# Queries and keys of the later batches: float32 loads on the sync queue, a ScalarE cast and a transposing DMA in place of TensorE transposes

## The chip, the cores and the metric

One Trainium2 chip, one of its cores. The metric is the device time of one execution in microseconds (us). Before the change the median of four runs is 342.4 us (339.9 to 343.6). The profiled execution of the kernel before took 346 us and was slow (slow means here that a run is over 1.5% above the fastest of the same kernel). The stretches of it used below all ran at a granted TensorE clock of 1.00, so I compare periods there and not its total. (The granted clock is the share of full speed that the chip's throttle gave TensorE.)

## The reference

Block-sparse attention, then a gated feed-forward layer on its output (4 batches, 8 heads, 768 tokens, head size 64):

```python
scores = scale * np.matmul(q, k.transpose(0, 1, 3, 2))
mask = ...        # neighbours, first and last block, 3 sampled blocks per block of 32
attn = softmax(np.where(mask, scores, -1e9))
x = (attn @ v)    # heads side by side: [3072, 512]
return ((sigmoid(x @ w_gate) * (x @ w_val)) @ w_out)
```

Queries and keys are normal with a spread of 0.1, so every score is tiny and the softmax is almost flat. **The comparison with the reference hardly sees the keys and queries**.

## The kernel before

Tokens lie 8 to a partition (`(p j)`, 96 partitions). A turn brings one pair of heads to [128 = two heads x 64, tokens]: 16 TensorE transposes into PSUM, then copies that put the tokens back in order.

```python
def load_qk(b, p, nm):                       # POOL queue, casts to float16 on the way
    t = work.tile([96, 2, PJ, D], f16, tag=f"{nm}16", bufs=KQ[nm])
    nc.gpsimd.dma_start(t..., src[b, 2*p:2*p+2].rearrange("h (p j) d -> p h (j d)", j=PJ))

def turn(b, p, nm):
    pt = ps.tile([128, PJ, 96], f16, tag="st", bufs=2)         # PSUM, shared with the scores
    for j in range(PJ):
        for hd in range(2):
            nc.tensor.transpose(pt[hd*D:hd*D+D, j, :], src[:, hd, j, :], ident[0:96, 0:96])
    tok = pt.rearrange("p j (b a) -> p b a j", a=4)            # neighbours are 96 elements apart
    if nm == "k":
        nc.vector.tensor_copy(kT..., tok)
        nc.scalar.copy(kb..., kT...)  # twice
    else:
        nc.scalar.copy(z[0:D, :, 0], tok[0:D])
        nc.vector.tensor_copy(z[D:128, :, 1], tok[D:128])

def spread_v(b, hh):                         # a burst: 12 DMAs on the sync queue
    for a in range(4):
        for s in range(3):
            nc.sync.dma_start(v4b[hh][32*s:32*s+32, a:NB:4], va[b % 2][32*a:32*a+32, ...])

def ahead(w):         # what window w prepares: two windows a pair of heads, 8 windows a batch
    b, i = divmod(w, 2 * NP)
    ...               # turn of a key pair, of a query pair; at i == 4 and i == 6 a burst
    # [cut]
```

`load_batch(b)` issues all loads of a batch at once. The main loop runs the feed-forward layer of one half batch while it interleaves the attention of the next. In the traces below each engine and each queue is seen to take its instructions in program order (a transpose whose data was ready at 155.5 us is issued at 159.86 us, after the copies placed before it); this matters most below.

The softmax here doesn't subtract the row's maximum and nothing guards it: scores larger than these inputs give would overflow.

## Time and profile before

| | |
|---|---|
| time | 342.4 us |
| PE busy | 295.9 us of 344.2 |
| one batch in the steady part (sixth to twelfth write of an output tile) | 72.5 us |
| TensorE in that part | 70.6 us busy, at clock 1.00 |

In profiles PE is TensorE and PEld its weight loads, DVE is VectorE, ACT ScalarE, POOL GpSimd and SPq the sync queue. The page's first part gives the busy time of each engine, its share of the span and its instructions:

```profile
PE 295.9 (86%) x3584; PEld 188.6 (55%) x3584; DVE 197.9 (57%) x363; ACT 167.0 (49%) x275; POOL 130.4 (38%) x133
```

The table of stretches, for one steady batch period (columns: stretch, its length, then busy us and number of instructions of PE, PEld, DVE, ACT, POOL, then the granted clock, the DMA share and GB/s):

```profile
166.50:239.00 72.50, 70.59 (x898) 44.89 (x897) 45.24 (x79) 38.69 (x68) 30.60 (x30) 1.00 0.57 99
```

TensorE is the limit there: 97% of the period, while ACT is busy for 53% and DVE for 62%. The timeline of TensorE around one turn (start, duration, what):

```profile
134.50 0.33 PE L361 MATMUL st<-qz,kT 128*128 128x128 f16 x3
134.76 0.53 PE L280 MATMUL ptr<-ident,k 96*64 96x96 f16 x16
135.22 0.39 PE L496 MATMUL py<-wo,h 128*128 128x512 f16 x1
```

The turn holds TensorE from 134.76 to 135.22 us, so 0.46 us. The groups of instructions (busy us, mean ns of one, then idle time before them and what ended it) give the copies out of PSUM and the projections:

```profile
L471 PE MATMUL gv<-x,wg 128*128 128x384 f16 x384 | 80.3, 333 | 0.0
...
L302 DVE COPY qz<-ptr 64x768 f16<-64x768 f16 x16 | 15.4, 961 | 5.7 <-ACT qz L301 5.4
L286 DVE COPY kT<-ptr 128x768 f16<-128x768 f16 x16 | 15.2, 954 | 2.9 <-PE ptr L280 2.7
L301 ACT COPY qz<-ptr 64x768 f16<-64x768 f16 x16 | 12.7, 794 | 11.3 <-PE ptr L280 11.3
```

The timeline of the sync queue shows the two bursts of one batch's preparation:

```profile
130.47 8.47 SPq L148 DMA_DIRECT2D v<-va  x12
...
141.45 0.34 SPq L510 DMA_DIRECT2D out_dram<-y  x1
141.89 8.36 SPq L148 DMA_DIRECT2D v<-va  x12
```

For 20 us the queue is nearly always issuing. Before the change nothing urgent stands behind that.

### The profile page before, as it was taken

How to read it: one execution, taken by the hardware profiler on the slowest of the kernel's cores; microseconds unless marked ns; L12 is line 12 of the kernel's file. 1: busy time of each engine (PE TensorE's matmuls, PEld its weight loads, DVE VectorE, ACT ScalarE, POOL GpSimd, SP SyncE). 2: the span in 40 equal slices, each digit the busy share in tenths (PEclk: the TensorE clock that was granted, in tenths of full speed). 3: DMA queues.
4: the chain of work that ended last, by engine and by line, in shares of the span. 5: the costliest groups of instructions: out<-in, count | busy, mean ns of one | idle time of the engine just before them, and what ended most of it. 6: DMA issues, size and time to landing. Idle time of an engine off the chain costs nothing.

```text
span 344.2 us, 8514 instructions
## 1 busy us (share of the span) xinstructions
PE 295.9 (86%) x3584; PEld 188.6 (55%) x3584; DVE 197.9 (57%) x363; ACT 167.0 (49%) x275; POOL 130.4 (38%) x133
## 2 busy tenths in 40 slices
PE   2143479697899999999999999999999999999994
PEld 2132365465556666566556656665566566655541
DVE  5985543477476655865585646665766545543321
ACT  7935334455265636465455536553665364522210
POOL 8543669544442775323143944340332400000000
PEclk9999957899899999999999999999999999999999
DMA  9999989997202499740102997510120000001002
GB/s 123 164 187 209 161 124 158 203 222 161 51 2 64 55 184 197 173 96 32 30 3 64 156 225 167 132 56 5 30 64 32 0 33 32 33 9 54 30 32 92
DMA packets 61319, 33.10 MB, mean 96 GB/s; under 512 B 28128, under 2 KB 57696, under 8 KB 61280
## 3 DMA queue, kind: packets, MB, share of 16 engines
q0 software_dynamic: 36368, 14.16, 35.1%
q1 hardware_dynamic: 24912, 18.39, 21.6%
q8 instruction: 28, 0.46, 0.6%
q14 instruction: 11, 0.09, 0.1%
HBM read 28.57 MB, written 6.29 MB: 101 GB/s over the span
## 4 chain that ended last, share of the span: by engine, by line
PE 68%; DVE 15%; ACT 9%; issue 5%; DMA 1%; POOL 0%; DVEq 0%; ACTq 0%; POOLq 0%
PE gv L471 32%; PE py L496 16%; PE st L361 9%; ACT pt L386 7%; PE pv L414 6%; PE ptr L280 3%; DVE pt L396 3%; DVE qz L302 3%; PE ptx L459 2%; DVE kT L286 2%; DMA k<-in_k_dram 1%; DVE h L482 1%; DVE xs L449 1%; DVE v L146 1%; DVE y L505 1%
## 5 line engine op out<-in xcount | busy, mean ns | idle before, releaser
L386 ACT ACTIVATE pt<-st 128x1024 f16<-128x1024 f32 (+2 forms) x96 | 82.1, 863 | 61.8 <-PE st L361 60.1
L396 DVE TENSOR_TENSOR pt<-pt,mask 128x1024 f16<-128x1024 f16 x64 | 52.6, 822 | 59.3 <-ACT pt L386 58.9
L471 PE MATMUL gv<-x,wv 128*128 128x384 f16 x384 | 80.1, 332 | 2.6 <-DVE h L482 2.6
L482 DVE SCALAR_TENSOR_TENSOR h<-tg,gv 128x384 f16<-128x384 f32 x96 | 53.0, 552 | 50.9 <-PE gv L471 43.6
L480 ACT ACTIVATE tg<-gv 128x384 f32<-128x384 f32 x96 | 46.9, 489 | 69.9 <-PE gv L471 69.9
L471 PE MATMUL gv<-x,wg 128*128 128x384 f16 x384 | 80.3, 333 | 0.0
L496 PE MATMUL py<-wo,h 128*128 128x512 f16 x288 | 72.7, 380 | 0.0
L312 POOL INDIRECT_COPY kg<-kT,idx 128x608 uint32 (+1 forms) x32 | 36.1, 1130 | 96.4 <-DVE h L482 25.3
L326 POOL INDIRECT_COPY vg<-v,idx 128x768 uint32 (+1 forms) x32 | 45.4, 1419 | 45.3 <-issue 23.1
L471 PEld LDWEIGHTS <-wv 128*128 128x128 f16 x384 | 38.1, 99 | 30.7 <-issue 7.5
L361 PE MATMUL st<-qz,kT 128*128 128x128 f16 (+1 forms) x192 | 36.6, 255 | 14.4 <-DVE qz L302 14.4
L471 PEld LDWEIGHTS <-wg 128*128 128x128 f16 x384 | 34.9, 99 | 20.2 <-issue 2.1
L496 PEld LDWEIGHTS <-h 128*128 128x128 f16 x288 | 25.4, 98 | 22.5
L414 PEld LDWEIGHTS <-pt 96*32 96x32 f16 (+2 forms) x1280 | 30.9, 103 | 6.7 <-ACT pt L386 1.0
L361 PE MATMUL st<-qz,kg 128*128 128x64 f16 x352 | 22.1, 200 | 4.6 <-POOL kg L312 2.8
L361 PE MATMUL st<-qz,kb 128*128 128x256 f16 (+1 forms) x96 | 25.9, 285 | 0.0
L414 PE MATMUL pv<-va,pt 128*64 128x65 f16 (+1 forms) x384 | 24.3, 200 | 0.8 <-ACT pt L386 0.8
L361 PEld LDWEIGHTS <-kg 128*128 128x128 f16 x352 | 19.2, 103 | 9.8 <-POOL kg L312 3.0
L505 DVE TENSOR_SCALAR y<-py 128x512 f32<-128x512 f32 x24 | 16.5, 689 | 8.6 <-PE py L496 8.6
L130 POOL DMA_DIRECT2D va<-in_v_dram x24 | 21.2, 906 | 0.0
L361 PEld LDWEIGHTS <-kb 128*128 128x128 f16 x96 | 9.9, 103 | 18.6 <-issue 13.9
L361 PEld LDWEIGHTS <-kT 128*128 128x128 f16 x192 | 15.9, 102 | 7.6 <-DVE qz L302 1.7
(56 smaller groups left out, 246.9 us busy)
## 6 DMA issues: line engine op xcount, KB each, us to landing
v<-va SPq DMA_DIRECT2D x90, 99.0 KB, 2.7
out_dram<-y SPq DMA_DIRECT2D x20, 256.0 KB, 2.0
k<-in_k_dram POOLq DMA_DIRECT2D x16, 192.0 KB, 5.4
va<-in_v_dram POOLq DMA_DIRECT2D x24, 128.0 KB, 5.6
q<-in_q_dram POOLq DMA_DIRECT2D x16, 192.0 KB, 5.7
wg<-in_moe_w_gate_dram POOLq DMA_DIRECT2D x3, 512.0 KB, 5.6
wv<-in_moe_w_val_dram POOLq DMA_DIRECT2D x3, 512.0 KB, 7.4
wo<-in_moe_w_out_dram POOLq DMA_DIRECT2D x3, 512.0 KB, 10.2
```

Source lines behind the costliest of these rows:

```text
L130: nc.gpsimd.dma_start(va[b % 2][:, m, :, 0:D], v[b, :, m * 128 : m * 128 + 128].rearrange("h p d -> p h d"),)
L312: nc.gpsimd.indirect_copy(words(t, BLK // 2)[:, 0:n], words(kT[b, p], BLK // 2), idx[:, half, 0 : 3 - half], i_know_this_is_slow=True,)
L326: nc.gpsimd.indirect_copy(words(t, VE // 2)[:, 0 : 2 * n, 0 : D // 2], words(v4[p // 2][:, p % 2 * 2 * VE : p % 2 * 2 * VE + 6528], D // 2 ...
L361: nc.tensor.matmul(st[:, col : col + n], keys, qs, start=True, stop=True)
L386: nc.scalar.activation(pt[:, 0:n], st[:, 0:n], AF.Exp, scale=SCALE)
L396: nc.vector.tensor_tensor(pp, pp, mk.unsqueeze(2).to_broadcast([128, nt, 2, nq]), op=ALU.mult)
L414: nc.tensor.matmul(pvv[rows, t % 3, hd, :], probs[w, x][0:k, c : c + n], val[:, 0:65], start=first[0], stop=False, skip_group_check=True, ...
L471: nc.tensor.matmul(t, w[:, i, f * 128 : (f + 1) * 128], xT[g, i], start=(i == 0), stop=(i == NP - 1),)
L480: nc.scalar.activation(tg, pgs.pop((g, f)), AF.Tanh, scale=0.5)
L482: nc.vector.scalar_tensor_tensor(h_, tg, 1.0, pvv_.pop((g, f)), op0=ALU.add, op1=ALU.mult)
L496: nc.tensor.matmul(pys[g, tt], hts[g, f][:, tt * 128 : (tt + 1) * 128], wo[:, f], start=(f == 0), stop=(f == NF - 1),)
L505: nc.vector.tensor_scalar_mul(y, pys.pop((g, tt)), 0.5)
```

## The change

It means to free TensorE of 24 of its 32 turns. Batches 1 to 3 are loaded as float32 by the sync queue, cast by ScalarE into pair order, and transposed by a DMA from SBUF to SBUF; load, cast and turn are one window apart. The core of the diff:

```diff
+    def load_raw(b, p, nm):
+        t = work.tile([96, 2, PJ, D], f32, tag="raw", bufs=4, name="raw")
+        nc.sync.dma_start(..., src[b, 2*p:2*p+2].rearrange("h (p j) d -> p h (j d)", j=PJ))
+    def flip(b, p, nm):
+        c = work.tile([96, PJ, 2, D], f16, tag="cast", bufs=2, name="cast")
+        nc.scalar.copy(c, raw.pop((nm, b, p)).rearrange("p h j d -> p j h d"))
+        t = work.tile([128, PJ, 96], f16, tag="turned", bufs=2, name="turned")
+        nc.sync.dma_start_transpose(t, c.rearrange("p j h d -> p (j h d)"))
     def turn(b, p, nm):
+        if b:
+            pt = turned.pop((nm, b, p))       # the copies below now read SBUF
+        else:                                 # as before
-            [128, 1024 if x < 2 else 640], f16, tag=f"pt{x // 2}", bufs=5 - x // 2, name="pt"
+            [128, 1024 if x < 2 else 640], f16, tag=f"pt{x // 2}", bufs=5 - 2 * (x // 2), name="pt"
     def ahead(w):
+        if i == 2 and b + 1 < B:
+            r.append(lambda: load_v(b + 1))
+        later(5, "k", turn); later(4, "k", flip); later(3, "k", load_raw)
         if b + 1 < B:
             if i == 4:
                 r.append(lambda: (spread_v(b + 1, 0), second_v(b + 1, 0)))
             if i == 6:
                 r.append(lambda: spread_v(b + 1, 1))
         # [cut]
+        later(7, "q", turn); later(6, "q", flip); later(5, "q", load_raw)
     # [cut: load_batch goes; before the main loop come load_v(1) and two load_raw]
```

## The prediction

> **What bounds the kernel now.** TensorE. The page gives PE 295.9 us busy of 344.2 (86%); the chain of waits is 68% PE. From 100 to 280 us the table of stretches shows PE busy 19.1 to 20.0 us of every 20, DVE 11 to 14, ACT 10 to 11; PE's own waits in 100 to 300 us sum to about 5 us. A half batch (projections of one half beside attention of the next) takes 36.2 us there. Idle PE lies mostly before 60 us, where batch 0 is prepared; that part keeps its TensorE transposes.
>
> **Removed.** 24 of 32 turns (16 transposes each). By the timeline a turn occupies 0.46 us of PE from its first start to the next instruction's (134.76 to 135.22, 144.60 to 145.06) in the PE-bound stretch: 24 x 0.46 = 11 us, the whole possible gain (3.2%). Also 24 cast loads on the POOL queue (not critical), and the PSUM slot each turn held until DVE (0.96 us) or ACT and DVE (0.79 + 0.96) had copied it.
>
> **Added.**
> - ACT: 24 casts of 96x1024 from float32. The zero cast in the trace takes 0.86 ns per element, so about 1.06 us each, 25 us in all (estimate); not a bound, but a cast can delay a tanh or exp that PE needs within 1 to 2 us: 2 to 4 us of PE stalls.
> - SP queue: 24 loads (0.6 us each, as its other issues) and 24 transposes. No trace shows a transposing DMA. The Trainium skill ("DMA: Bandwidth & Descriptors", Latency and other measured facts) gives 261 GB/s as effective, so 192 KB moves in under 1 us beside the 2 to 3 us which the trace shows for any SP copy; estimate 3 to 5 us to landing, 1 to 2 us of issue.
> - DVE: the same copies, now from SBUF. The skill ("VectorE: DVE Perf Modes", What auto-detection actually checks) lets a single-source SBUF copy run at 2x; kT copies may fall from 0.96 to 0.5 us.
>
> **The critical point is the order on the SP queue.** Per batch it already issues two bursts of 12 value copies and 3 more (130.5 to 150.2 us). A turn follows its cast by 5 to 9 us, but the transpose of the second key pair queues behind the first burst, the first query pair's behind the second. I work out landings 0 to 4 us late in each place. DVE and ACT run in order, so a late turn holds h and tanh, and PE stops 1 to 2 us later. Six such places give back 0 to 15 us; middle, about 4.
>
> **Sum.** 343 - 11 + 3 (casts) + 4 (late turns) - 1 (DVE and PSUM relief) = 338 us. Range 327 (no stalls) to 354 (transposes of 6 us or more). Faster by over 2%: 0.40; within 2%: 0.34; slower by over 2%: 0.26.
>
> **What would show each step.** PE busy down some 15 us by the page's overlapping count, ptr matmuls 512 to 128; ACT busy up 25 us; transposes landing in 3 to 5 us; half-batch period 34.5 to 36 us. Stalls show as DVE kT or ACT and DVE qz copies waiting on the transposing DMA, and PE gv waiting on DVE h, at 75 to 90, 140 to 155 and 210 to 225 us.
>
> **What would make it wrong.** A transpose that costs much more on the SP queue or in the DMA engines (every turn late, y stores too: 360 us or more); a transpose under 2.5 us with a light burst (331); ACT waits for raw loads held behind the bursts.

## The result

| | before | the change |
|---|---|---|
| median of 4 runs | 342.35 us | 384.17 us |
| range | 339.9 to 343.6 | 383.3 to 386.3 |

The ratio is 1.124 (95% interval 1.116 to 1.132), so the change is 12% slower. Here and below a ratio is the mean time of one kernel's fast runs over that of the other's of the same rounds, so it is not quite the ratio of the medians quoted. The outputs are right.

The page's first part, and the groups that answer to those shown before, all of the change:

```profile
PE 299.4 (78%) x3200; PEld 186.6 (49%) x3200; DVE 192.9 (50%) x363; ACT 193.4 (51%) x299; POOL 118.9 (31%) x109
```

```profile
L496 PE MATMUL gv<-x,wg 128*128 128x384 f16 x384 | 85.8, 350 | 6.0 <-ACT tg L505 5.8
...
L145 ACT CAST cast<-raw 96x1024 f16<-96x1024 f32 x24 | 24.9, 1038 | 4.1 <-DMA raw<-in_q_dram 2.8 <-DMA raw<-in_k_dram 1.3
...
L326 ACT COPY qz<-turned 64x768 f16<-64x768 f16 x12 | 18.0, 1503 | 9.2 <-DMA turned<-cast 9.2
...
L327 DVE COPY qz<-turned 64x768 f16<-64x768 f16 x12 | 12.2, 1014 | 6.7 <-DMA turned<-cast 6.4
...
L311 DVE COPY kT<-turned 128x768 f16<-128x768 f16 x12 | 10.5, 871 | 15.0 <-DMA turned<-cast 15.0
```

Three things stand out. The 384 transposes (24 turns of 16) are gone from PE's count, and yet PE is busy 3.5 us longer: the same projection matmul takes 350 ns and not 333. ScalarE's query copy takes 1.50 us from SBUF against 0.79 us from PSUM. And the copies now wait for the transposing DMA. Its own cost is not to blame: it lands in a median of 3.1 us and holds the queue for 1.26 us, as predicted.

The sync queue of the change in the preparation of batch 2, by its timeline:

```profile
149.73 8.06 SPq L170 DMA_DIRECT2D v<-va  x12
...
159.15 0.60 SPq L180 DMA_DIRECT2D vb<-va  x1
159.86 1.75 SPq L147 DMA_TRANSPOSE turned<-cast  x1
161.71 0.53 SPq L535 DMA_DIRECT2D out_dram<-y  x1
162.29 0.41 SPq L137 DMA_DIRECT2D raw<-in_k_dram  x1
...
169.53 9.06 SPq L170 DMA_DIRECT2D v<-va  x12
178.70 1.30 SPq L147 DMA_TRANSPOSE turned<-cast  x1
180.04 0.58 SPq L137 DMA_DIRECT2D raw<-in_q_dram  x1
```

What the engines do meanwhile, from the timeline of all engines (in brackets: idle time before, and what ended it):

```profile
154.44 1.03 ACT L145 CAST cast<-raw 96x1024 f16<-96x1024 f32 x1
...
163.42 0.81 DVE L311 COPY kT<-turned 128x768 f16<-128x768 f16 x1 [3.35 <-DMA turned<-cast]
164.26 0.46 ACT L316 COPY kb<-kT 128x320 f16<-128x320 f16 x1 [4.98 <-DVE kT L311]
166.52 1.04 ACT L145 CAST cast<-raw 96x1024 f16<-96x1024 f32 x1 [0.52 <-DMA raw<-in_k_dram]
167.56 0.49 PE L484 MATMUL ptx<-ident,xs 128*128 128x128 f16 x3 [3.96 <-ACT cast L145]
...
181.56 1.49 ACT L326 COPY qz<-turned 64x768 f16<-64x768 f16 x1 [2.65 <-DMA turned<-cast]
184.07 1.04 ACT L145 CAST cast<-raw 96x1024 f16<-96x1024 f32 x1 [0.63 <-DMA raw<-in_q_dram]
185.02 0.69 ACT L411 ACTIVATE pt<-st 128x640 f16<-128x640 f32 x1
185.77 0.32 PE L439 MATMUL pv<-va,pt 128*64 128x65 f16 x3 [3.58 <-ACT pt L411]
```

Read it from the top. The cast is done at 155.5 us, but the queue is in its first burst and the three value copies behind it, so the transpose is issued at 159.86 and VectorE, which had come to the key copy, stands until 163.42. ScalarE stands behind VectorE for 4.98 us, and TensorE for 3.96 us. (The bracket names the cast, which ended last by the profile's count; the operand itself, `xs`, is VectorE's, written at 167.5 us behind that same key copy.) The second burst does it again, with one more link: the load issued at 180.04 holds a cast until 184.07, behind that cast stands an exp, and TensorE stands 3.58 us for the exp. Each such wait is short because the one before it has already eaten the time.

A stop costs TensorE more than its length. The table of stretches around the second stop, again of the change (the clock is the third number from the end):

```profile
180.00:185.00 5.00, 2.19 (x24) 1.35 (x21) 1.50 (x2) 2.81 (x3) 1.43 (x1) 0.97 0.94 208
185.00:190.00 5.00, 3.35 (x44) 2.27 (x45) 1.11 (x3) 0.93 (x3) 0.00 (x0) 0.50 0.56 121
190.00:195.00 5.00, 5.00 (x26) 2.50 (x25) 2.53 (x4) 0.85 (x3) 0.00 (x0) 0.85 0.15 38
```

The Trainium skill ("TensorE: Matmul & The Clock Gate", the part on the HAM clock gate) says that an idle window of about 3.4 us drops the array to half its clock until it has been busy for about as long. This trace agrees that a stop halves the clock, but not in both lengths: in the stop of 3.58 us the granted clock falls to 0.50 at 184.7 us, 2.5 us after the stop began, and stays there for 6.8 us, to 191.5 us; a stop of 3.08 us, from 267.77 us, does the same. Over the period 192.20 to 277.40 us, which holds the preparation of batch 3 with stops of 4.09 and 3.08 us in the same two places, the clock is 0.92, where before it is 1.00.

The period from the sixth to the twelfth output tile, read off VectorE's timeline, goes from 72.5 us (166.52 to 238.97) to 85.2 us (192.23 to 277.44), 12.8 us more. It holds the preparation of batch 3; the stops shown above, of batch 2, lie before it. Three batches are prepared this way, and 3 x 12.8 = 38 us is nearly the whole difference of 42 us. (The sixth tile, after two preparations, already comes 25.7 us later, twice 12.8; that figure leans on the slow profile of the kernel before.) After the last preparation nothing differs: from the twelfth to the eighteenth tile both take 69 us.

### The profile page after: what moved, and what is told of

Same layout as the page of the kernel before. It is cut to its first block, busy times and chain, and to the rows that moved or that the text cites. A ratio compares the mean times of both kernels' runs of the same rounds, so it can differ in the third digit from the quotient of the medians.

```text
span 382.6 us, 7839 instructions
## 1 busy us (share of the span) xinstructions
PE 299.4 (78%) x3200; PEld 186.6 (49%) x3200; DVE 192.9 (50%) x363; ACT 193.4 (51%) x299; POOL 118.9 (31%) x109
## 4 chain that ended last, share of the span: by engine, by line
PE 45%; DVE 15%; DMA 13%; ACT 12%; issue 8%; SPq 5%; POOL 0%; DVEq 0%; ACTq 0%; POOLq 0%
PE gv L496 21%; PE py L521 12%; ACT pt L411 7%; DMA turned<-cast 7%; PE st L386 5%; PE pv L439 4%; DMA raw<-in_q_dram 3%; DVE kT L311 3%; DVE qz L327 3%; SPq L170 2%; DVE pt L421 2%; PE ptx L484 2%; DVE xs L474 2%; SPq L147 1%; DMA pair<-in_k_dram 1%
## 5 line engine op out<-in xcount | busy, mean ns | idle before, releaser
L496 PE MATMUL gv<-x,wg 128*128 128x384 f16 x384 | 85.8, 350 | 6.0 <-ACT tg L505 5.8
L496 PE MATMUL gv<-x,wv 128*128 128x384 f16 x384 | 84.2, 345 | 4.0 <-DVE h L507 3.9
L421 DVE TENSOR_TENSOR pt<-pt,mask 128x1024 f16<-128x1024 f16 x64 | 47.2, 739 | 57.0 <-ACT pt L411 57.0
L521 PE MATMUL py<-wo,h 128*128 128x512 f16 x288 | 75.8, 392 | 0.0
L496 PEld LDWEIGHTS <-wg 128*128 128x128 f16 x384 | 37.5, 104 | 31.9 <-issue 13.9
L439 PE MATMUL pv<-va,pt 128*64 128x65 f16 (+1 forms) x384 | 25.2, 204 | 12.8 <-ACT pt L411 12.8
L484 PE MATMUL ptx<-ident,xs 128*128 128x128 f16 x96 | 12.5, 249 | 25.5 <-DVE xs L474 21.5
L145 ACT CAST cast<-raw 96x1024 f16<-96x1024 f32 x24 | 24.9, 1038 | 4.1 <-DMA raw<-in_q_dram 2.8
L316 ACT COPY kb<-kT 128x320 f16<-128x320 f16 x16 | 7.3, 457 | 31.0 <-DVE kT L311 31.0
L326 ACT COPY qz<-turned 64x768 f16<-64x768 f16 x12 | 18.0, 1503 | 9.2 <-DMA turned<-cast 9.2
L484 PEld LDWEIGHTS <-xs 128*128 128x128 f16 x96 | 6.9, 106 | 31.9 <-DVE xs L474 30.6
```

The costliest lines, as they stand in the source:

```text
L145: nc.scalar.copy(c, raw.pop((nm, b, p)).rearrange("p h j d -> p j h d"))
L421: nc.vector.tensor_tensor(pp, pp, mk.unsqueeze(2).to_broadcast([128, nt, 2, nq]), op=ALU.mult)
L439: nc.tensor.matmul(pvv[rows, t % 3, hd, :], probs[w, x][0:k, c : c + n], val[:, 0:65], start=first[0], stop=False, skip_group_check=True, ...
L484: nc.tensor.transpose(pt[:, t, :], x[:, t, :], ident)
L496: nc.tensor.matmul(t, w[:, i, f * 128 : (f + 1) * 128], xT[g, i], start=(i == 0), stop=(i == NP - 1),)
L521: nc.tensor.matmul(pys[g, tt], hts[g, f][:, tt * 128 : (tt + 1) * 128], wo[:, f], start=(f == 0), stop=(f == NF - 1),)
```

## The experiments

Theory A: the loads, casts and transposes are late, because loads and transposes stand behind the bursts on the sync queue. Theory B: the added work itself (25 us of casts, slower copies, DMA traffic) costs. All times are medians; the ratio is to the kernel before in the same rounds. "Period" is the sixth to twelfth output tile of the profiled run; in brackets where that run was slow.

| run | what | us | ratio | period |
|---|---|---|---|---|
| before | | 342.4 | | 72.5 |
| change | | 384.2 | 1.124 | 85.2 |
| e1 | turns wait for no transpose (wrong result) | 380.1 | 1.122 | 84.1 |
| e2 | no loads, casts, transposes (wrong result) | 340.3 | 0.998 | 71.7 |
| e3 | casts, but TensorE transposes | 354.5 | 1.043 | 74.6 |
| e4 | bursts in pieces | 350.2 | 1.031 | 72.8 |
| e5 | e2, copies in source order | 374.0 | 1.101 | 82.0 |
| e6 | e4 + e5's copies + later weight load | 384.4 | 1.129 | 86.0 |
| e7 | float32 loads on the POOL queue | 390.5 | 1.145 | 81.3 |
| e8 | e1 + e7 (wrong result) | 376.6 | 1.098 | (81.2) |
| e9 | e2, contiguous copies (wrong result) | 331.3 | 0.974 | 68.8 |
| e10 | e4 + later weight load | 346.6 | 1.014 | (73.1) |
| e11 | e10 + tokens loaded so that copies are contiguous | 346.1 | 1.017 | 71.3 |
| e12 | e11 with casting POOL loads | 341.6 | 1.001 | 69.4 |
| e13 | all work done, nothing waits for it (wrong result) | 342.6 | 1.005 | 72.5 |
| e14 | e12 for batches 2 and 3 only | 335.4 | 0.986 | 69.7 |
| e15 | before, with 8 wide TensorE transposes | 353.2 | 1.033 | 75.1 |

### First round: e1 to e4

e1 lets every later turn read one fixed tile; the transposes go into a tile nobody reads (here, in e8 and in e13 with one buffer in place of two). e2 has in addition a bare `return` in `load_raw` and `flip`, so loads, casts and transposes are gone.

```diff
-            pt = turned.pop((nm, b, p))
+            pt = fixed                        # filled once, from batch 0
```

> Wrong result on purpose: every later turn reads one fixed tile (real data of batch 0), while the loads, casts and transposing DMAs all still run, into a tile that nobody reads. Theory A (turns wait for transposes that land late behind the bursts on the SP queue): the waits on the transposing DMA go, so most of the loss goes: 335 to 350 us. Theory B (the added ScalarE work, 25 us of casts and 9 us of slower query copies, delays exp and tanh): nothing of that changes, so 370 us or more.

Measured 380.1 us. Read naively, theory A is dead. But the waits of e1 (us in all, times, longest) show that the time merely moved one link up:

```profile
ACT cast L146 <- DMA raw<-in_k_dram: 14.6, 4, 4.1
ACT cast L146 <- DMA raw<-in_q_dram: 12.7, 5, 4.3
```

In the change the casts waited 4.1 us in all for their loads; here it is 27 us. The loads stand behind the same bursts, and a cast that waits holds ScalarE just as well as a late turn. So e1 did not separate the theories.

> Wrong result on purpose: as e1, but no loads, casts or transposing DMAs of queries and keys after the first batch at all. What is left is TensorE without its 24 turns and the copies from SBUF. Theory A and B both expect the whole possible gain: about 331 us (343 less 11). If it stays above 350, something else in the change costs (the slower ScalarE copy from SBUF, the smaller buffer pool, the moved value loads).

Measured 340.3 us: no gain at all, although TensorE had 11 us less to do. Neither theory expected that; the text had named the slower copies as one candidate. e5 and e9 follow it up.

e3 keeps the loads and casts and transposes the cast tile with TensorE:

```diff
-        nc.sync.dma_start_transpose(t, c.rearrange("p j h d -> p (j h d)"))
+                    nc.tensor.transpose(pt[hd*D:hd*D+D, j, :], src[:, j, hd, :], ident[0:96, 0:96])
```

> The float32 loads and ScalarE casts stay, but TensorE transposes the cast tile as before, so no transposing DMA and copies from PSUM. Correct result. Theory A: near before plus a few us of casts, 343 to 352 us. Theory B: the casts alone cost most of it, 365 us or more.

Measured 354.5 us, a little over the range of A and far under B's. The period is 2.1 us longer than before; one wait of a cast for its load, 6.8 us, lies in the start.

e4 changes only what the sync queue issues when. Each burst becomes pieces, and the three extra value copies move to the last window of the batch:

```diff
-            if i == 4:
-                r.append(lambda: (spread_v(b + 1, 0), second_v(b + 1, 0)))
-            if i == 6:
-                r.append(lambda: spread_v(b + 1, 1))
+        if b + 1 < B and i >= 4:
+            hh, a0 = divmod(i - 4, 2)
+            pieces = [lambda a=a: spread_v(b + 1, hh, part=(a,)) for a in (2 * a0, 2 * a0 + 1)]
+        # at i = 4, 5 around the gathers; at i = 6, 7 after the query's flip and load
```

> The change with its value-copy bursts cut in pieces of 3 DMAs, spread over four windows and placed so that each transposing DMA finds at most two pieces ahead of it; everything else as in the change. Correct result. Theory A: the late turns of the second key pair and first query pair are no longer late, 350 to 365 us. Theory B: about 380 us.

Measured 350.2 us, 34 us won back by order alone, with every byte, cast and transpose still there. Its sync queue, for comparison with that of the change:

```profile
138.17 3.87 SPq L170 DMA_DIRECT2D v<-va  x6
142.86 1.24 SPq L147 DMA_TRANSPOSE turned<-cast  x1
144.15 0.58 SPq L137 DMA_DIRECT2D raw<-in_k_dram  x1
145.49 0.37 SPq L535 DMA_DIRECT2D out_dram<-y  x1
145.90 4.64 SPq L170 DMA_DIRECT2D v<-va  x6
```

The period is 72.8 us, 12.4 less than the change's. A 8.8 us stop of TensorE is left in the preparation of batch 1, where a transpose lands after 11.8 us beside the output-weight loads.

### Second round: e5 to e8

e5 (on top of e2) and e6 (on top of e4) walk the copies in the order of their source; e6 also issues the output-weight loads later, as e10 below:

```diff
-            nc.scalar.copy(z[0:D, :, 0], tok[0:D])
+            nc.scalar.copy(zj[0:D, 0], pj[0:D])     # reads neighbours, writes 8 elements apart
```

> e2 (wrong result on purpose: one fixed tile, no loads, casts or transposing DMAs) with the copies out of the turned tile walked in the order of their source, so that they read neighbouring elements. e2 came out at 340 us and not at 331; in the change the ScalarE query copy takes 1.50 us from SBUF against 0.79 us from PSUM. If that strided read from SBUF is what ate the floor's gain, the copy falls to about 0.85 us and the run to 330 to 336 us. If not, 339 to 341 us, and the loss sits elsewhere.

> e4 (split bursts, 350 us) with the copies of e5 and with the three output-weight loads moved from before the first group to the fifth to seventh window, because in e4 one transposing DMA took 11.8 us to land beside them and TensorE stood 8.8 us. Correct result. If order on the SP queue, that collision and the slow copy are the whole loss: 332 to 338 us. If the casts and the DMA traffic cost more than that: 341 us or more.

Both missed, in the wrong direction: 374.0 and 384.4 us. Neighbouring reads were bought with scattered writes, and those are far worse. The group of instructions in e5:

```profile
L327 ACT COPY qz<-fixed 64x768 f16<-64x768 f16 x12 | 41.8, 3483 | 0.0
L305 DVE COPY kT<-fixed 128x768 f16<-128x768 f16 x12 | 27.0, 2250 | 0.0
```

As a mend it failed, but it is a clean measurement of something else: 24 us more on ScalarE (12 x 1.97) and 27 us more on VectorE made e2 34 us longer, with TensorE's work unchanged. Both engines are only half busy; their time counts all the same, because what TensorE waits for stands behind it.

e7 moves the float32 loads to the POOL queue, e8 does e1 and e7 together:

```diff
-        nc.sync.dma_start(        # in load_raw
+        nc.gpsimd.dma_start(
```

> The change with only its float32 loads moved from the SP queue to the POOL queue; bursts as in the change. Correct result. Casts then no longer wait behind bursts, but the transposes still do. If the two ways of being late (cast waits for its load, turn waits for its transpose) cover for each other, this alone helps little, as e1 alone did: 368 to 382 us. If late loads were the one cause: about 345 us.

> e1 and e7 together (wrong result on purpose: turns read a fixed tile; float32 loads on the POOL queue). Neither casts nor turns can then wait behind a burst, with all work still done. If lateness behind the bursts is the cause: 340 to 352 us. If the added load on ScalarE and the DMA engines is: 370 us or more.

e7 was even slower than the change (390.5 us) and over its range; its steady period is 81.3 us, 4 less than the change's, but it loses more before that, up to the sixth tile. e8 came to 376.6 us, near what theory B expected (two of its four runs are slow; the fast ones took 371.3 and 376.1 us). But its waits, in a slow profile, again show casts held: 14.3 us for the transposing DMA, because a cast needs a buffer that a transpose still reads, and 13.0 us for loads that now stand on the POOL queue between its gathers (the copies that collect the sampled blocks). The two runs therefore settle nothing between A and B; they show how many ways the chain has to be late.

### Third round: e9 to e12

e9 is e2 with copies that read and write neighbours, and so leave the tokens in a wrong order:

```diff
-            nc.scalar.copy(z[0:D, :, 0], tok[0:D])
+                pj = pt.rearrange("p j n -> p (j n)").rearrange("p (b r) -> p b r", r=BLK)
+                nc.scalar.copy(zz[0:D, :, 0], pj[0:D])      # VectorE's two copies likewise
```

> e2 (wrong result on purpose, one fixed tile, nothing loaded or transposed) with copies that read and write neighbouring elements (tokens in a wrong order, also on purpose). e5 showed that walking the copies in source order makes their scattered writes far slower (3.48 us) and the run 34 us longer, so copies on ScalarE and VectorE do count. If the scattered 2-byte reads of the change (1.50 us) ate the gain in e2: copies near 0.86 us on ScalarE and 0.5 us on VectorE, and 328 to 335 us. If not: 338 to 341 us.

Measured 331.3 us, ratio 0.974: nearly the whole possible gain that the prediction had worked out (10 of 11 us by the medians; 3.7 of 3.7 us a period). Its copies, by group, with those of e2 after them:

```profile
L325 ACT COPY qz<-fixed 64x768 f16<-64x768 f16 x12 | 9.9, 824 | 0.0
...
L305 DVE COPY kT<-fixed 128x768 f16<-128x768 f16 x12 | 5.7, 477 | 0.0
```

```profile
L319 ACT COPY qz<-fixed 64x768 f16<-64x768 f16 x12 | 18.1, 1510 | 0.0
...
L304 DVE COPY kT<-fixed 128x768 f16<-128x768 f16 x12 | 13.0, 1087 | 0.0
```

So reading single float16 elements 192 bytes apart from SBUF ate the gain of the freed TensorE: 71.7 against 68.8 us a period. (Before the change ScalarE read at the same distance from PSUM in 0.79 us. e9's copies on VectorE are shorter than those before the change too, 0.48 against 0.95 us, so its gain is that of freed turns and short copies together.)

e10 moves only the output-weight loads of e4, out of the way of the first transposes (`if 5 <= w < 8: load_wo(w - 5)` in `ahead`); e11 loads tokens `(j p)`, so that the transposing DMA delivers them in order and, for keys, straight into their final tile; e12 has the POOL queue load and cast:

```diff
-            src[b, 2*p:2*p+2].rearrange("h (p j) d -> p h (j d)", j=PJ),
+            src[b, 2*p:2*p+2].rearrange("h (j p) d -> p (h j) d", j=PJ),     # e11: rows of 256 bytes
-        nc.scalar.copy(c, raw.pop((nm, b, p)).rearrange("p h j d -> p j h d"))
+            nc.gpsimd.dma_start(t[:, :, hd], src[b, 2*p+hd].rearrange("(j p) d -> p j d", j=PJ))  # e12
```

> e4 (split bursts, 350 us) with only the output-weight loads moved to the fifth to seventh window; copies as in the change. Correct result. e4 lost 8.8 us where a transposing DMA took 11.8 us beside those loads: 340 to 346 us if that collision is the cause, 349 to 352 us if the stall only moves.

> e10 with tokens loaded so that the transposing DMA gives them in order: loads of 256-byte rows, keys transposed straight into their final tile (no VectorE key copy), query copies of neighbouring elements. Casts stay on ScalarE. Correct result. Worked out per batch of 72.4 us before: less 3.7 for TensorE, plus about 2 for the casts, nothing for copies: 334 to 341 us; above 345 us if the loads of short rows come late.

> e11 without ScalarE casts: the POOL queue loads with a cast as before the change, two DMAs a tile, straight into pair order; the sync queue then only transposes. Correct result. If the casts and copies are all that is left of the loss: 330 to 337 us, better than before. If the POOL queue's extra issues delay its gathers: 340 us or more.

e10: 346.6 us, a little over its range; of the 8.8 us stop, 3.6 us were won in the median (6 us by the ratios, which leave out e10's slow run), and several stops of 2 to 3 us took its place. e11: 346.1 us, above its range, by the branch that the expectation named: its casts waited 15.5 us for the queries' short-row loads. e12, which also takes back the smaller probability pool, as e14 does: 341.6 us, equal to before. Its steady period is 69.4 us, 3 better than before, but it loses that in the preparation of batch 1, with stops of TensorE of 4.0 and 4.5 us.

### Fourth round: e13 to e15

By then the prediction was known to be wrong and no run had cleanly separated lateness from load. e13 does: everything is still loaded, cast and transposed, in the order of the change, and nothing waits for it.

```diff
-            pt = turned.pop((nm, b, p))
+            pt = fixed
-        nc.scalar.copy(c, raw.pop((nm, b, p)).rearrange("p h j d -> p j h d"))
+        nc.scalar.copy(c, some...)            # same shape, read from the weights as float32
-        nc.sync.dma_start_transpose(t, c.rearrange("p j h d -> p (j h d)"))
+        nc.sync.dma_start_transpose(t, still.rearrange("p j h d -> p (j h d)"))
```

> The change with all its added work done and nothing waiting for it (wrong result on purpose): turns read one fixed tile, casts read other data that is long there, the transposing DMAs read a fixed tile and write one that nobody reads, the float32 loads land in tiles that nobody reads; order on every queue as in the change. If lateness (casts and turns held behind the bursts) is the cause of what e4 won: e2's 340 us plus some 6 us for the casts, 343 to 351 us. If the added work itself (ScalarE, DMA traffic) is: 370 us or more.

Measured 342.6 us, even a little under the range. Its row for one period:

```profile
163.50:236.00 72.50, 66.46 (x770) 41.95 (x769) 43.24 (x78) 46.80 (x76) 25.55 (x22) 1.00 0.84 142
```

The row to hold beside it is that of the change:

```profile
192.20:277.40 85.20, 71.83 (x769) 44.10 (x768) 44.85 (x78) 47.44 (x76) 26.23 (x22) 0.92 0.69 121
```

Same matmuls, same ScalarE work, but 12.7 us between them, 13.4 us of idle TensorE (85.2 less 71.8) against 6.0, and clock 0.92 against 1.00. So lateness is the cause of the loss, as theory A has it. Of theory B's list, casts, loads and transposes together cost 0.8 us a period (72.5 against e2's 71.7); the slower copies, which e2 has too, cost the 2.9 us that e9 shows, and that is most of what the freed TensorE gains. e4, where every dependence is in place, has a period of 72.8 us: nearly all of the 12.7 us goes away by the order of the sync queue alone.

e14 keeps TensorE's transposes for batch 1 and does e12's for batches 2 and 3:

```diff
-                if 0 <= p < NP and 0 < b2 < B:
+                if 0 <= p < NP and 0 < b2 < B and (b2 > 1 or f is turn):
-        if b:
+        if b > 1:                             # in turn
+    load_qk(1, 0, "k"); load_qk(1, 0, "q"); load_v(1); ...      # batch 1 as before
```

> e12 for batches 2 and 3 only; batch 1 is loaded and transposed by TensorE as before. Correct result. In e12 the period from batch 1's to batch 2's first stored edge tile was 67.8 us against 72.4 us before, but batch 1, prepared beside the weight loads, stood still for some 15 us. If that is all: 341 less twice 4.6, 330 to 335 us, faster than before by 2 to 3%. If a transposing DMA is late in the other batches too: 338 us or more.

Measured 335.4 us, ratio 0.986 (0.983 to 0.989): the one right version that beats both kernels, by 1.4%, a little short of the range. The interval is clear of 1. The 67.8 us that the expectation quotes was read off the issue of stores, which the sync queue itself shifts; by the writes of output tiles e12's period is 69.4 us, so the gain to be had was 3 and not 4.6 us a batch.

e15 asks whether TensorE can be spared otherwise: the loads of the kernel before are written in pair order, so that 8 transposes of 128 columns do.

> The rival way to save TensorE time: before, with its cast loads written into pair order (two DMAs a tile on the POOL queue), so that a turn is 8 transposes of 128 columns instead of 16 of 64; no transposing DMA. Correct result. A turn should fall from 0.46 us to about 0.3 us of TensorE: 336 to 340 us; above 342 us if short-row writes make the loads late.

Measured 353.2 us, a miss. The loads now take two issues a tile on the POOL queue, which is in order too: it issues loads from 54.5 to 74.2 us, a gather stands behind them, and TensorE stands 14.3 us for that gather. What the wide transposes are worth was not separated from that.

## Why the prediction was wrong

**Right.** The place: "the transpose of the second key pair queues behind the first burst, the first query pair's behind the second", with VectorE's key copy and both query copies waiting for the transposing DMA. The cost of that DMA (3.1 us to land, 1.26 us of issue). The possible gain: 11 us, of which e9 shows 10. The casts' length (1.04 us; 1.06 had been estimated, in part by luck: the rate it was said to come from, 0.86 ns for each of 1024 elements, gives 0.88).

**Wrong, the step that decides: "Six such places give back 0 to 15 us; middle, about 4."** Measured, lateness costs 12.7 us a period (the change less e13) and 41.5 us over the whole run by the medians (384.2 less 342.6), ten times the middle. The single waits were foreseen fairly (five of the key copy, at most 4.6 us, and four of ScalarE's query copy, at most 3.2 us, where six of 0 to 4 us had been worked out); what TensorE loses by them was not. Three things were left out of that term. The lateness was worked out for the transposes alone, but the loads stand behind the same bursts, so casts wait too, and the next transpose is later for it (27 us of waits appear in e1 as soon as the other link is cut); the prediction had this only among what could make it wrong. A wait on VectorE or ScalarE was counted as if it ended when the tile landed, while exp, tanh and the normalization that stood behind it still had to run before TensorE could go on (read off the timeline above, not tested alone). And stops of 3 to 4 us cost clock: 0.92 over the period. By the two rows above, TensorE idles 7.3 us longer than in e13, and the same number of matmuls keeps it busy 5.4 us longer (71.8 against 66.5), at the lower clock.

**Wrong in sign: "- 1 (DVE and PSUM relief)".** I took from the Trainium skill ("VectorE: DVE Perf Modes", What auto-detection actually checks) that a copy from SBUF may run at twice the rate, and did not ask how far apart its elements lie. The key copy fell from 0.95 to 0.87 us and not to 0.5, and ScalarE's query copy rose from 0.79 to 1.50 us. e2 less e9 puts the scattered reads at 2.9 us a period, 9 us over the run by the medians (340.3 less 331.3), where a gain of 1 had been expected. The page "SBUF — State Buffer" of the skill, in the note on cachelines under Door 1, says that accesses which cross to a new 16-byte line pay a penalty; the runs agree (1.50 us for reads 192 bytes apart, 0.82 us for neighbours).

**About right: "+ 3 (casts)".** With nothing late, casts, loads and transposes together cost 0.8 us a period and 2.3 us over the run (e13's 342.6 less e2's 340.3, not clear of noise). Where TensorE keeps its turns and so has less room, in e3, loads and casts cost 2.1 us a period.

In one line, per period: 72.5 - 3.7 (eight turns) + 2.9 (scattered reads) + 0.8 (added work) + 12.7 (late) = 85.2, as measured. The last three terms are differences between one run and the next (e9, e2, e13, the change), so they must add up; what the sum tests is its first step, 68.8 us, which e9 meets.

**A check that was read wrongly in advance: "PE busy down some 15 us".** It rose by 3.5 us. Busy time is counted at whatever clock is granted, so a kernel that makes TensorE wait can show more of it. The mean length of one matmul form (350 against 333 ns) tells the two apart.

What stays open: how the 12.7 us divide between late loads and late transposes. e1, e7 and e8 each left another link late, so no run separates them. The cost of moving the value loads and of the smaller probability pool was not tested alone; e13 has both, and with them only 0.8 us over e2, which has both as well; e9, which also has both, reached the full gain, so neither costs much there. Why VectorE's key copy takes 0.87 us in the change and 1.09 us in e2, with the same distances, is not known.

## What to carry to other kernels

Before putting a short, urgent DMA on a queue, read what that queue issues in the preceding ten microseconds: here reordering one queue was worth 34 us and the DMA itself almost nothing. When a chain of load, cast, transpose and copy crosses several in-order queues, removing one wait only exposes the next; the run that decides leaves all the work in and takes every dependence away, and a run that only reorders (e4) confirms it. An engine that is half busy is not free if what the bottleneck engine waits for stands behind its work, and the distance between elements decides what a copy costs there.

## What the Trainium skill lacked or had wrong

- "SBUF — State Buffer", note on cachelines, says that crossing 16-byte lines costs but not how much; no page says it for ScalarE, or for VectorE with 2-byte elements. The runs: ScalarE copies 64x768 float16 in 0.82 us with neighbouring reads and writes, 1.50 us with reads 192 bytes apart, 3.48 us with writes 16 bytes apart; VectorE's 128x768 copy takes 0.48, 1.09 (0.87 in the change) and 2.25 us.
- "VectorE: DVE Perf Modes", What auto-detection actually checks, names the conditions of the double rate; it does not say there that scattered elements take the gain away, though the closing rules of the page ask for dense data (0.87 us against 0.95 us from PSUM, where neighbours reach 0.48 us).
- "DMA: Bandwidth & Descriptors", Latency and other measured facts, gives a bandwidth for the transposing DMA, but no time for a single one, and no page has the time of one of this size. Here one of 192 KB lands in a median of 3.1 us (2.8 to 10.7) and holds the sync queue for 1.26 us, twice as long as one of the value copies there (0.61 us).
- No page that I read has the order of a queue as a cost: twelve small copies hold the sync queue for 8 to 9 us, and a transpose behind them starts that much later.
- "TensorE: Matmul & The Clock Gate", the part on the HAM clock gate, gives about 3.4 us of idleness before the clock halves and about as much work before it returns. Here a stop of 3.08 us was enough, and after it and after one of 3.58 us the clock came back 6.8 us after it fell (3.4 us after one of 3.96 us).
